# Frequency 0 as a bias in the last inverse transform's evictions: four products per row block instead of five

## The chip, the cores and the metric

The kernel runs on one core of a Trainium2 chip. The metric is the device time of one execution in microseconds; before the change the median of three runs is 128.48 us (128.36 to 128.61). In the profile PE is the matrix engine (TensorE), PEld its weight loads, DVE VectorE, ACT ScalarE, POOL GpSimd, and SP the engine that only issues transfers.

## The reference

The input x has 2048 rows (s) of 512 numbers (d). The output mixes two branches with one gate per row:

```python
    g = _sigmoid((x * gate_w).sum(-1, keepdims=True))
    a = _A_ref(x, A_w_r, A_w_i)
    b = _B_ref(x, B_w1, B_b1, B_w2, B_b2)
    return g * a + (1 - g) * b
```

Branch a is a spectral filter: a real 2-D Fourier transform over s and d, a product with a complex weight for each frequency pair (2048 x 257), and the inverse transform. Branch b is a token-mixing MLP: a layer norm over d, a product over s to 1792 hidden units, a gelu, a product back to 2048 rows with bias b2.

## The kernel before

All 2048 rows stay in SBUF as 16 blocks of 128 rows; block j = 4q + r holds the rows 512q + 4a + r. Fourier transforms are done as products with cosine and sine tables on TensorE, with radix-4 butterflies on VectorE around them, so that only short tables are needed. The MLP's products are m1 (line 727, x to hidden units, 14 tiles `ft`) and m2 (line 993, hidden units back to rows, 14 products of 128x512 per row block).

The stages in order: layer norm and the forward transform over s (i.e. fa, lines 584 to 587) between m1 products; the forward transform over d (fb, lines 692 to 695); the multiplication by the weights on VectorE; the inverse transform over s (i1, lines 893 to 900), between m2 products; a butterfly (fq, lines 928 and 929) that writes its result z in two halves h into the tile `xp` (`xph(0)` and `xph(1)`); and the last inverse transform, over d (i3, lines 975 to 979), for each row block j.

i3 uses the symmetry of cosines and sines: for a row block it makes four pieces in one PSUM bank: the even frequencies along d (h = 0) and the odd ones (h = 1) each give a cosine part and a sine part, for the first quarter of the columns d, from which the others follow by symmetry. The cosine part of h = 0 has 129 columns, the others 127, 128 and 128, 512 in all. The part v = 0 of z holds real parts, v = 1 imaginary parts. Frequencies 0 and 256 along d have no imaginary part, so frequency 256 is kept in the place of frequency 0's imaginary part. That is why the 129-column piece takes two products: one of the real parts with the cosine table, and a second, of the imaginary parts with a table in which only the row of frequency 256 is not zero (`g[:, 512:641]`).

The PSUM tiles of i3 alternate between the tags `fa` and `fb`, each with two buffers. ACT evicts each (i3ev, line 983), multiplying by the row's gate `g`, into a pair tile of `E` (`epair`, five pairs). Then VectorE adds and subtracts the pieces (`es`, `fold`, lines 998 to 1004) to get 512 outputs per row. For the first 14 row blocks ACT evicts m2's result with scale 1 − g and bias (1 − g) b2 (yev, line 1009; the four PSUM buffers of tag `acc`), and VectorE adds the two branches for a pair of blocks (`fin`, line 1023). For blocks 14 and 15 `es` adds the bias itself to the 129 columns of the cosine part (line 1028), and VectorE reads m2's result directly (`fin`, line 1035). A transfer on SP stores each group of rows.

The order of instructions isn't written by hand. Each step is a task with an engine, an estimated duration, what it reads and writes and a priority (`add`); `Plan.order` plays through the tasks with these estimates and emits them in the order in which they would start. So another estimate moves m2 products to other places between the transform's products. On each engine instructions run in that order. Transfers of SP and ACT use eight semaphore lanes; a ninth waits for the first on its lane.

Of the kernel before, what the change touches and what calls it, by code (L numbers as in the profile page):

```python
# [12 lines left out]
Alu = mybir.AluOpType  # L13
# [22 lines left out]
def make_tables():  # L36

    p = np.arange(P)
    r4 = np.arange(4)
    alt = np.where(p % 2 == 0, 1.0, -1.0)  # L40

    def ang(rows, k, n):
        return 2 * np.pi * ((rows[..., None] * k) % n) / n

    ta = np.zeros((P, 4, 640))
    ti = np.zeros((P, 2946))
    for r in range(4):
        s = 4 * p + r
        for n, k0 in enumerate((0, 2)):
            th = ang(s, k0 + 4 * np.arange(64), S)  # L50
            ta[:, r, n * 128:n * 128 + 64] = np.cos(th)
            ta[:, r, n * 128 + 64:n * 128 + 128] = -np.sin(th)
        ta[:, r, 64] = alt
        th = ang(s, 1 + 4 * p, S)
        ta[:, r, 256:384] = np.cos(th)
        ta[:, r, 384:512] = -np.sin(th)
        ta[:, r, 512:640] = -np.cos(th)

        k = 4 * (p % 64) + 2 * (p // 64)
        o, w = ti_at(r)  # L60
        v = ti[:, o:o + w]
        if r % 2:
            sg = np.where(p < 64, 1.0, -1.0)[:, None]
            th = ang(k, s, S)
            v = v.reshape(P, 7, P)
            v[:, 0] = np.cos(th)
            v[:, 1] = sg * np.cos(th)
            v[:, 2] = -np.sin(th)
            v[:, 3] = -sg * np.sin(th)
            v[0, 2:4] = alt * (0.5 ** 0.5 if r == 1 else -(0.5 ** 0.5))  # L70
            th = ang(1 + 4 * p, s, S)
            v[:, 4] = -np.sin(th)
            v[:, 5] = np.cos(th)
            v[:, 6] = np.sin(th)
            ti[:, o:o + w] = v.reshape(P, w)
        else:
            s5 = np.append(s, 512)
            for lt, kk in enumerate((k, 1 + 4 * p)):
                th = ang(kk, s5, S)
                c, n = np.cos(th), -np.sin(th)  # L80
                if lt == 0:
                    n[0, 0:P] = 0.0 if r == 0 else -alt
                u = v[:, 256 * lt:256 * lt + 256]
                u[:, 0:P], u[:, P:] = c[:, 0:P], n[:, 0:P]
                if r == 0:
                    u[:, P] = c[:, P] if lt == 0 else -n[:, P]
    ti[0, 2816:2945] = np.append(alt, 1.0)

    tb = np.zeros((P, 3, 4, 64))
    i = np.arange(64)  # L90
    for b in (0, 2):
        th = ang(p, b + 4 * i, D)
        tb[:, 0, b // 2] = np.cos(th)
        tb[:, 1, b // 2] = -np.sin(th)
    tb[:, 1, 0, 0] = alt
    tb[:, 2, 0:2] = tb[:, 0, 0:2]
    tc = np.zeros((P, 2, 3, 2, 64))
    for n, b in enumerate((1, 3)):
        th = ang(p, b + 4 * i, D)
        sg = 1.0 if b == 1 else -1.0  # L100
        tc[:, 0, 0, n] = np.cos(th)
        tc[:, 0, 1, n] = -np.sin(th)
        tc[:, 1, 0, n] = -sg * np.sin(th)
        tc[:, 1, 1, n] = -sg * np.cos(th)
    tc[:, :, 2] = tc[:, :, 0]
    cf = np.zeros((P, 4, 2))
    m = np.arange(8).reshape(4, 2)
    for r in range(4):
        cf[m[0, 0], r, 0] = 1.0
        cf[8, r, 0] = (1.0, -1.0)[r % 2]  # L110
        cf[m[1, r % 2], r, 0] = (1.0, -1.0, -1.0, 1.0)[r]
        if r != 2:
            cf[m[2, 0], r, 1], cf[m[3, 0], r, 1] = 1.0, (1.0, -1.0)[r % 2]
        if r != 0:
            cf[m[2, 1], r, 1], cf[m[3, 1], r, 1] = (0.0, -1.0, 1.0, 1.0)[r], (0.0, -1.0, -1.0, 1.0)[r]
    tb = np.concatenate([tb[:, :, 0:2].reshape(P, 384), tc.reshape(P, 768), cf.reshape(P, 8)], 1)

    tg = np.zeros((P, 642))
    sc = 2.0 / (D * S)
    d = np.arange(129)  # L120
    for h in range(2):
        th = ang(2 * p + h, d, D)
        c, n = sc * np.cos(th), -sc * np.sin(th)
        if h == 0:
            c[0], n[0] = sc / 2, 0.0
            tg[:, 0:129], tg[:, 129:256] = c, n[:, 1:128]
        else:
            tg[:, 256:384], tg[:, 384], tg[:, 385:512] = c[:, 0:128], -n[:, 128], n[:, 1:128]
    tg[0, 512:641] = np.where(d % 2 == 0, 1.0, -1.0) * sc / 2
    m, e = np.arange(P)[:, None], np.arange(3, -1, -1)  # L130
    ix = np.zeros((P, 2, 4))
    ix[:, 0] = 512 * e + 256 + np.where(m < 64, 4 * (64 - m), 4 * (127 - m) + 2)
    ix[0, 0] = (0, 1536, 1792, 1280)
    ix[:, 1] = 512 * e + 4 * (127 - m) + 3
    return {"ta": bf(ta), "ti": bf(ti), "tb": bf(tb), "tg": bf(tg), "tn": bf(np.eye(NFT)), "ix": ix.reshape(P, 8).astype(np.int32)}
# [142 lines left out]
def kernel(  # L278
# [39 lines left out]
    def dma(out_ap, in_ap, eng=None):  # L318
        (eng or nc.sync).dma_start(out=out_ap, in_=in_ap)
# [158 lines left out]
    def ld_ti():  # L478
        t["ti"] = sb([P, 2946], BF16, "rot")
        dma(t["ti"][:], tabs["ti"], nc.gpsimd)  # L480
    load("tg", [P, 642], BF16, tabs["tg"], (P, 1284), prio=120, eng="POOL", reads=[("hold", 3)])


    OWN = {0: (0, 8, 4, 12), 1: (1, 5), 2: (2,), 3: (3,)}
# [304 lines left out]
    for lt in range(2):  # L789
# [8 lines left out]
        if lt == 0:  # L798
            def nyq():
                pz = sb([1, 1280], F32, "X")  # L800
                na = pz[:, 0:1024].rearrange("p (i v l) -> p i v l", i=2, v=2)
                nn = t["nn"] = pz[:, 1024:1280].bitcast(BF16).rearrange("p (v l) -> p v l", v=2)
                wn, v = t["wn"], t["B"][0:1, 0, 0, 2:4, :]
                for i in range(2):
                    V.tensor_mul(na[:, i], v, wn[:, i, None, 0:L].to_broadcast([1, 2, L]))
                V.tensor_sub(nn[:, 0], na[:, 0, 1], na[:, 1, 0])
                V.tensor_add(nn[:, 1], na[:, 1, 1], na[:, 0, 0])
                V.tensor_mul(nn[:, :, 0], t["c0"][0:1, 0, 0, 1, :], wn[:, 0, 0:257:256])
            add("DVE", 3 * d1(512) + 0.1, nyq, reads=bk + [("W", 0), ("W", 1), ("c0", 0)] + pbk, writes=["nn"], prio=0.5)

        def c0b(lt=lt):
# [35 lines left out]
        add("DVE", tt(2048) + 2 * tt(1024), ob, reads=["xs"], writes=bk, prio=pr)  # L847

        def c0c(lt=lt):
            V.tensor_copy(t["B"][:, lt, :, :, 0], t["ce"][:, lt].rearrange("p e c k -> p e (c k)"))  # L850
        add("DVE", 0.15, c0c, reads=[("ce", lt)], writes=bk, prio=pr)

        if lt == 0:
# [76 lines left out]
        add("DVE", 2 * tt(2048), fq, reads=[("zz", h, r, lt) for r in range(4) for lt in range(2)] + [("T", 0, 0), ("T", 0, 1), ("T", 1, 0), ("T", 1, 1)], writes=["xs" if h == 0 else "pp", ("z", h)], prio=3.6)  # L930


    for i in range(NW):
        n = (0, 3, 5)
        if i in n:
            k = n.index(i)

            def w2alloc(k=k):
                t["w2", k] = sb([P, 6, S], BF16, "wa") if k == 0 else sb([P, 4, S], BF16, "wb", 2)
            add("SP", 0.01, w2alloc, writes=[("w2a", k)], prio=31 + i, alloc=["wa" if k == 0 else "wb"])  # L940

        def ldw2(i=i):
            w, o = w2at(2 * i)
            dma(w[:, o:o + 2, :], w2v[:, 2 * i:2 * i + 2, :])
        add("SP", 0.43, ldw2, reads=[("w2a", k)], writes=[("w2", i)], prio=31 + i, pk=(256, 5200))

    def w2at(ft):
        k = w1of(ft)
# [17 lines left out]
    for grp in groups:  # L966
        for j in grp:
# [3 lines left out]
            def i3(j=j, q=q, r=r, tag=tag):  # L971
                p3 = t["i3", j] = ps([P, 2, L], F32, tag, 2)
                g = t["tg"]
                zv = [xph(h).rearrange("p (q v r a) -> p q v r a", q=4, v=2, r=4)[:, q, :, r, :] for h in range(2)]
                T.matmul(p3[:, 0, 0:129], lhsT=zv[0][:, 0], rhs=g[:, 0:129], start=True, stop=False)
                T.matmul(p3[:, 0, 0:129], lhsT=zv[0][:, 1], rhs=g[:, 512:641], start=False, stop=True)
                T.matmul(p3[:, 0, 129:256], lhsT=zv[0][:, 1], rhs=g[:, 129:256], start=True, stop=True)
                T.matmul(p3[:, 1, 0:128], lhsT=zv[1][:, 0], rhs=g[:, 256:384], start=True, stop=True)
                T.matmul(p3[:, 1, 128:256], lhsT=zv[1][:, 1], rhs=g[:, 384:512], start=True, stop=True)
            add("PE", mm(*[129] * 5), i3, reads=[("z", 0), ("z", 1), "tg"], writes=[("i3", j)], prio=4, alloc=[tag])  # L980

            def i3ev(j=j):
                A.activation(epair(j // 2 % NEO)[:, j % 2], t["i3", j][:], ActF.Copy, scale=t["g"][:, j:j + 1])  # L983
            i3e = add("ACT", act(512, 1), i3ev, reads=[("i3", j), "g"], writes=[("eo", j)], prio=1.5, alloc=["eo"] if j % 2 == 0 else (), free=[tag],
                      after=[i3e] if j % 2 else ())
            parts = [slice(0, D)] if j < NJ - 1 else [slice(0, 384), slice(384, D)]
            for n, cs in enumerate(parts):
# [37 lines left out]
            else:  # L1025
                def es(j=j, fold=fold, quart=quart):
                    e, s = epair(j // 2 % NEO)[:, j % 2], espair()[:, :, 0:2]
                    V.tensor_scalar_add(e[:, 0, 0:129], e[:, 0, 0:129], t["ombb2"][:, j:j + 1])
                    fold(e, quart(tbuf(j)[:, None]), s)
                add("DVE", tiny(1) + 4 * tt(256) + 0.15, es, reads=[("eo", j), "omg"], writes=[("o", j)], prio=4, free=["eo"] if j % 2 else (), after=gates)  # L1030

                for n, cs in enumerate(parts):
                    def fin(j=j, n=n, cs=cs):
# [46 lines left out]
```

## Time and profile before

| | |
|---|---|
| median of 3 runs | 128.48 us (128.36 to 128.61) |
| the profiled execution | 128.45 us, its span 126.5 us |
| PE busy | 121.8 us, 746 products |
| DVE busy | 109.2 us |
| ACT busy | 81.4 us, 170 instructions |
| i3: L975 to L979 | 80 products, from 98.09 us on |
| i3ev: L983 | 16 of 128x512, about 0.71 us each |
| yev: L1009 | 14 of 128x512, 0.78 us each |
| the last four products of i1 (L893) | from 93.34 us on |
| the last eight products of PE (L993) | from 123.16 us on |

A span is the time from the first to the last recorded instruction; the execution's time holds 1.95 us more. Rows of the timeline give the start, the time from the first start to the last end, engine, line, operation, tiles and shapes, and the count of merged instructions. Matmuls follow each other before the one ahead has left the array, and ACT's instructions overlap too, so the step from one start to the next says what one costs its engine; the duration says when its result is there.

### The profile page before, as it was taken

The numbers are of one execution on the slowest core, as the hardware profiler recorded it, in microseconds if no ns is written. First come the engines' busy times: TensorE is split into PE (matmuls) and PEld (weight loads), VectorE is DVE, ScalarE is ACT, GpSimd is POOL, SyncE is SP. The second block draws the span as 40 slices with busy tenths as digits, with TensorE's granted clock in tenths as the row PEclk, the third lists the DMA queues.
The fourth block names the chain that finished last, engine by engine and source line by source line (L and its number), as shares of the span: only waits on it lengthen the run. The fifth ranks groups of instructions, "written<-read, shape, count | busy, mean of one in ns | idle before, by whom it ended". The sixth has DMA issues, their size and how long they took to land.

```text
span 126.5 us, 2104 instructions
## 1 busy us (share of the span) xinstructions
PE 121.8 (96%) x746; PEld 69.3 (55%) x759; DVE 109.2 (86%) x240; ACT 81.4 (64%) x170; POOL 28.0 (22%) x38
## 2 busy tenths in 40 slices
PE   6999999999999999999999999999999999999991
PEld 2455545565444476644455545557675776555570
DVE  1799999999999999999999999996597399999431
ACT  3799996999988889984220064228992999622200
POOL 6902638787778400000000000000000000000000
PEclk9999999999999999999999999999999999999999
DMA  4999999999999999991029600000000004213131
GB/s 99 323 349 369 364 369 364 335 337 341 296 211 207 341 392 416 408 387 56 0 21 372 274 0 0 0 3 8 0 0 0 5 0 166 95 71 139 47 110 41
DMA packets 15059, 23.14 MB, mean 183 GB/s; under 512 B 1496, under 2 KB 12138, under 8 KB 15050
## 3 DMA queue, kind: packets, MB, share of 16 engines
q1 hardware_dynamic: 13338, 19.70, 47.4%
q0 software_dynamic: 1232, 2.91, 7.1%
q10 hardware_dynamic: 480, 0.40, 0.9%
q8 instruction: 6, 0.10, 0.4%
q14 instruction: 3, 0.02, 0.1%
HBM read 20.90 MB, written 2.10 MB: 182 GB/s over the span
## 4 chain that ended last, share of the span: by engine, by line
PE 92%; DMA 3%; ACT 1%; issue 1%; SPq 0%; DVE 0%
PE acc L993 37%; PE acc L727 32%; PE fb L727 5%; DMA wa<-in_B_w_dram 3%; PE fb L695 1%; PE fa L587 1%; PE fa L893 1%; PE fa L586 1%; PE fb L893 1%; PE fa L695 1%; PE fa L584 1%; PE fa L585 1%; PE fa L993 1%; ACT X L983 1%; PE fa L692 0%
## 5 line engine op out<-in xcount | busy, mean ns | idle before, releaser
L993 PE MATMUL acc<-gl,wb 128*128 128x512 bf16 (+1 forms) x124 | 31.1, 376 | 0.1
L727 PE MATMUL acc<-h,wb 128*128 128x512 bf16 x124 | 28.6, 379 | 0.2
L993 PE MATMUL acc<-gl,wa 128*128 128x512 bf16 (+1 forms) x94 | 24.0, 376 | 0.2
L993 PEld LDWEIGHTS <-wb 128*128 128x128 bf16 x136 | 14.7, 114 | 10.6 <-issue 0.2
L727 PEld LDWEIGHTS <-wb 128*128 128x128 bf16 x128 | 12.5, 98 | 13.9
L1009 ACT ACTIVATE x<-acc,ombb,omg 128x512 bf16<-128x512 f32 x14 | 10.7, 776 | 14.7 <-PE acc L993 14.7
L727 PE MATMUL acc<-h,wa 128*128 128x512 bf16 (+1 forms) x66 | 16.7, 366 | 0.2 <-DMA wa<-in_B_w_dram 0.2
L993 PEld LDWEIGHTS <-wa 128*128 128x128 bf16 x102 | 11.1, 113 | 8.4
L727 PEld LDWEIGHTS <-wa 128*128 128x128 bf16 x102 | 9.8, 98 | 9.0 <-DMA wa<-in_B_w_dram 1.0
L747 ACT ACTIVATE gl<-acc,b1f 128x512 bf16<-128x512 f32 x12 | 8.0, 690 | 7.6 <-PE acc L727 7.6
L494 DVE BATCH_NORM_STATS2 stats<-x 128x6 f32<-128x512 bf16 x12 | 8.2, 682 | 2.2 <-DMA x<-in_A_x_dram 2.2
L467 POOL DMA_INDIRECT W<-in_A_w_r_dram,ix x8 | 9.4, 1171 | 2.4 <-issue 2.4
L763 ACT ACTIVATE x<-x 128x512 bf16<-128x512 bf16 x16 | 9.9, 621 | 0.0
L727 PE MATMUL fb<-h,wa 128*128 128x512 bf16 (+1 forms) x33 | 9.6, 366 | 0.1
L590 ACT CAST X<-fa 128x512 bf16<-128x512 f32 x16 | 9.0, 575 | 1.1 <-PE fa L587 0.9
L467 POOL DMA_INDIRECT W<-in_A_w_i_dram,ix x8 | 8.8, 1101 | 2.4 <-issue 2.4
L555 ACT ACTIVATE h<-x,nmr,rstd 128x512 bf16<-128x512 bf16 x8 | 6.4, 806 | 0.0
L864 ACT CAST s<-fa 8x512 bf16<-8x512 f32 x1 | 0.6, 574 | 8.3 <-PE fa L862 8.3
L983 ACT ACTIVATE X<-fb,g 128x512 bf16<-128x512 f32 x8 | 5.7, 708 | 0.0
L983 ACT ACTIVATE X<-fa,g 128x512 bf16<-128x512 f32 x8 | 5.6, 706 | 0.0
L699 ACT CAST B<-fa 128x512 bf16<-128x512 f32 x8 | 5.0, 624 | 0.6 <-PE fa L695 0.6
L1023 DVE TENSOR_TENSOR x<-x,X 128x1024 bf16<-128x1024 bf16 x7 | 4.6, 685 | 0.8 <-ACT x L1009 0.8
(177 smaller groups left out, 245.7 us busy)
## 6 DMA issues: line engine op xcount, KB each, us to landing
wb<-in_B_w_dram SPq DMA_DIRECT2D x8, 512.0 KB, 12.7
wb<-in_B_w_dram SPq DMA_DIRECT2D x4, 1024.0 KB, 8.7
wa<-in_B_w_dram SPq DMA_DIRECT2D x3, 1024.0 KB, 10.7
wa<-in_B_w_dram SPq DMA_DIRECT2D x2, 768.0 KB, 8.6
out_dram<-x SPq DMA_DIRECT2D x3, 512.0 KB, 3.7
x<-in_A_x_dram SPq DMA_DIRECT2D x2, 512.0 KB, 9.3
wa<-in_B_w_dram SPq DMA_DIRECT2D x4, 192.0 KB, 4.2
wa<-in_B_w_dram SPq DMA_DIRECT2D x2, 384.0 KB, 5.0
```

What stands on the lines that cost most here:

```text
L467: add("POOL", 1.0, lambda lt=lt, e=e: nc.gpsimd.indirect_dma_start(out=W()[:, lt, e, 1, 0:257], out_offset=None, in_=w, in_offset=bass.Ind ...
L494: V.bn_stats(out=t["stats"][:, j, :], in_=t["x"][:, j // 4, j % 4, :])
L555: add("ACT", act(512, 2), lambda j=j: A.activation(t["h"][:, j // 4, j % 4, :], t["x"][:, j // 4, j % 4, :], ActF.Identity, bias=t["nmr"][ ...
L590: add("ACT", act(512), lambda r=r, dq=dq: A.copy(t["X"][:, :, r, :, dq, :], t["pa", r, dq][:]), reads=[("pa", r, dq)], writes=[("X", r, dq ...
L699: A.copy(t["B"][:, lt, e, 2 * c:2 * c + 2, :].rearrange("p s (i b) -> p s i b", b=4), t["pb", lt, e, c][:].rearrange("p s b i -> p s i b"))
L727: T.matmul(t["u", ft][:, cs], lhsT=w[:, j // 4, j % 4, c * P:(c + 1) * P], rhs=t["h"][:, j // 4, j % 4, cs], start=(j == jorder[0] and not ...
L747: gelus.append(add("ACT", act(512, 1), lambda ft=ft: A.activation(t["gl"][:, ft, :], t["u", ft][:], ActF.Gelu_apprx_tanh, bias=t["b1f"][:, ...
L763: A.activation(t["x"][:, q, r, :], t["x"][:, q, r, :], ActF.Copy, accum_out=t["glog"][:, 4 * q + r:4 * q + r + 1])
L983: A.activation(epair(j // 2 % NEO)[:, j % 2], t["i3", j][:], ActF.Copy, scale=t["g"][:, j:j + 1])
L993: T.matmul(t["y", j, n][:, cs], lhsT=w[:, o, 512 * q + r:512 * q + 512:4], rhs=t["gl"][:, ft, cs], start=(ft == 0), stop=(ft == NFT - 1))
L1009: A.activation(tbuf(j).rearrange("p h d -> p (h d)"), t["y", j, 0][:], ActF.Identity, bias=t["ombb2"][:, j:j + 1], scale=t["omg"][:, j:j + 1])
L1023: V.tensor_add(o, o, epair(NEO + 1 + j // 2 % NOB))
```

## The change

Frequency 256 takes the place of frequency 0 in the first row of the cosine table, so that the 129-column piece needs one product. For that the two change places in z: the copies of the lines' end values (`c0c`) and the row of frequency 1024 along s (`nyq`) are written in reversed order. What frequency 0 along d adds is the same number in all 129 columns of a row's cosine part. It is brought into one number per row: a transfer (`dcl`, 4 x 512 from one partition of `xph(0)` to the tile `dc`), four small products with a unit matrix that turn it into columns (`dct`), and two VectorE operations (`dcs`) that multiply by the gate and, for blocks 14 and 15, add the bias of b2. ACT's eviction becomes two: 383 columns with scale g as before, and the 129 columns of the cosine part with scale g and bias `dcb`. Line 1028 goes. The w2 tiles 1 and 2 come in one transfer instead of two.

In the new order TensorE's instructions are the same up to the last L893; after it come 11 products of line 993, `dct`, 8 more, four i3 blocks in a row, and then the other twelve blocks after 5, 3, 3, 3, 3, 7, 3, 3, 7, 3, 3 and 7 products of line 993. Before, it was 20 products, four blocks, and then one or two products between blocks for most of them. On VectorE, each pair's `es` is followed by its `fin`; before, two of the one came ahead of two of the other.

```diff
-    tg = np.zeros((P, 642))
+    tg = np.zeros((P, 512))
...
-            c[0], n[0] = sc / 2, 0.0
+            c[0], n[0] = np.where(d % 2 == 0, 1.0, -1.0) * sc / 2, 0.0
...
-    tg[0, 512:641] = np.where(d % 2 == 0, 1.0, -1.0) * sc / 2
...
-                V.tensor_mul(nn[:, :, 0], t["c0"][0:1, 0, 0, 1, :], wn[:, 0, 0:257:256])
+                V.tensor_mul(nn[:, ::-1, 0], t["c0"][0:1, 0, 0, 1, :], wn[:, 0, 0:257:256])
...
-            V.tensor_copy(t["B"][:, lt, :, :, 0], t["ce"][:, lt].rearrange("p e c k -> p e (c k)"))
+            V.tensor_copy(t["B"][:, lt, :, :, 0].rearrange("p e (c v) -> p e c v", c=2)[:, :, :, ::-1], t["ce"][:, lt])
...
+    def dcl():
+        t["dc"] = sb([4, D], BF16, "dc")
+        dma(t["dc"][:], xph(0)[0:1].rearrange("p (q v n) -> p q v n", q=4, v=2)[:, :, 1], DCE)
+    DCE = None
+    add("SP", 0.5, dcl, reads=[("z", 0)], writes=["dc"], prio=0, pk=(4, 1024, 4))
+
+    def dct():
+        pd = t["pdc"] = ps([P, 4, 4], F32, "fb", 2)
+        for r in range(4):
+            T.matmul(pd[:, r], lhsT=t["dc"][:, r * P:(r + 1) * P], rhs=t["tn"][0:4, 0:4], start=True, stop=True)
+    add("PE", 0.2, dct, reads=["dc", "tn"], writes=["pdc"], prio=2.9, alloc=["fb"])
+
+    def dcs():
+        v = lambda name: t[name][:].rearrange("p (q r) -> p r q", r=4)
+        t["dcb"] = sb([P, NJ], F32, "dcb")
+        V.scalar_tensor_tensor(v("dcb"), t["pdc"][:], 1.0 / (D * S), v("g"), op0=Alu.mult, op1=Alu.mult)
+        V.tensor_add(t["dcb"][:, 14:16], t["dcb"][:, 14:16], t["ombb2"][:, 14:16])
+    add("DVE", 0.25, dcs, reads=["pdc", "g", "omg"], writes=["dcb"], prio=1, free=["fb"], after=gates)
+
-    for i in range(NW):
+    for i, e in ((0, 1), (1, 3), (3, 4), (4, 5), (5, 6), (6, NW)):
...
-                T.matmul(p3[:, 0, 0:129], lhsT=zv[0][:, 0], rhs=g[:, 0:129], start=True, stop=False)
-                T.matmul(p3[:, 0, 0:129], lhsT=zv[0][:, 1], rhs=g[:, 512:641], start=False, stop=True)
+                T.matmul(p3[:, 0, 0:129], lhsT=zv[0][:, 0], rhs=g[:, 0:129], start=True, stop=True)
...
-            add("PE", mm(*[129] * 5), i3, reads=[("z", 0), ("z", 1), "tg"], writes=[("i3", j)], prio=4, alloc=[tag])
+            add("PE", mm(*[129] * 4), i3, reads=[("z", 0), ("z", 1), "tg"], writes=[("i3", j)], prio=4, alloc=[tag])
...
-                A.activation(epair(j // 2 % NEO)[:, j % 2], t["i3", j][:], ActF.Copy, scale=t["g"][:, j:j + 1])
-            i3e = add("ACT", act(512, 1), i3ev, reads=[("i3", j), "g"], writes=[("eo", j)], prio=1.5, alloc=["eo"] if j % 2 == 0 else (), free=[tag],
+                e = epair(j // 2 % NEO)[:, j % 2].rearrange("p h d -> p (h d)")
+                v = t["i3", j][:].rearrange("p h d -> p (h d)")
+                A.activation(e[:, 129:], v[:, 129:], ActF.Copy, scale=t["g"][:, j:j + 1])
+                A.activation(e[:, 0:129], v[:, 0:129], ActF.Identity, bias=t["dcb"][:, j:j + 1], scale=t["g"][:, j:j + 1])
+            i3e = add("ACT", act(383, 1) + act(129, 2), i3ev, reads=[("i3", j), "g", "dcb"], writes=[("eo", j)], prio=1.5, alloc=["eo"] if j % 2 == 0 else (), free=[tag],
...
-                    V.tensor_scalar_add(e[:, 0, 0:129], e[:, 0, 0:129], t["ombb2"][:, j:j + 1])
```

More of the change, by code (lines that the diff above doesn't have):

```diff
@@ L480, in ld_ti @@
         dma(t["ti"][:], tabs["ti"], nc.gpsimd)
-    load("tg", [P, 642], BF16, tabs["tg"], (P, 1284), prio=120, eng="POOL", reads=[("hold", 3)])
+    load("tg", [P, 512], BF16, tabs["tg"], (P, 1024), prio=120, eng="POOL", reads=[("hold", 3)])
     OWN = {0: (0, 8, 4, 12), 1: (1, 5), 2: (2,), 3: (3,)}
@@ L940, with ldw2 @@
             add("SP", 0.01, w2alloc, writes=[("w2a", k)], prio=31 + i, alloc=["wa" if k == 0 else "wb"])
-        def ldw2(i=i):
+        def ldw2(i=i, n=2 * (e - i)):
             w, o = w2at(2 * i)
-            dma(w[:, o:o + 2, :], w2v[:, 2 * i:2 * i + 2, :])
-        add("SP", 0.43, ldw2, reads=[("w2a", k)], writes=[("w2", i)], prio=31 + i, pk=(256, 5200))
+            dma(w[:, o:o + n, :], w2v[:, 2 * i:2 * i + n, :])
+        add("SP", 0.43, ldw2, reads=[("w2a", k)], writes=[("w2", m) for m in range(i, e)], prio=31 + i, pk=(256 * (e - i), 5200))
     def w2at(ft):
@@ L1027, in es @@
                     e, s = epair(j // 2 % NEO)[:, j % 2], espair()[:, :, 0:2]
-                    V.tensor_scalar_add(e[:, 0, 0:129], e[:, 0, 0:129], t["ombb2"][:, j:j + 1])
                     fold(e, quart(tbuf(j)[:, None]), s)
-                add("DVE", tiny(1) + 4 * tt(256) + 0.15, es, reads=[("eo", j), "omg"], writes=[("o", j)], prio=4, free=["eo"] if j % 2 else (), after=gates)
+                add("DVE", tiny(1) + 4 * tt(256), es, reads=[("eo", j)], writes=[("o", j)], prio=4, free=["eo"] if j % 2 else (), after=gates)
                 for n, cs in enumerate(parts):
```

## The prediction

> **What bounds the kernel now.** I read the page first, then the chain of waits, then the timeline of the stretch that the diff touches, and last the rows that price its new instructions.
>
> ```profile
> span 126.5 us, 2104 instructions
> PE 121.8 (96%) x746; PEld 69.3 (55%) x759; DVE 109.2 (86%) x240; ACT 81.4 (64%) x170; POOL 28.0 (22%) x38
> ...
> PE 92%; DMA 3%; ACT 1%; issue 1%; SPq 0%; DVE 0%
> ```
>
> TensorE ends the chain nearly everywhere. A 96% average can hide a stage with another limit, so the table by stretches for the last third:
>
> ```profile
> 98.10:107.50 9.40, 9.24 (x102) 6.90 (x103) 7.11 (x22) 9.40 (x17) 0.00 (x0) 1.00 0.14 58
> 107.50:123.80 16.30, 16.22 (x89) 9.20 (x88) 11.95 (x36) 4.38 (x7) 0.00 (x0) 1.00 0.23 89
> ```
>
> After the length come PE, PEld, DVE, ACT, POOL with counts, then the granted clock. In the first stretch, where the last transform runs, two engines are full: PE with 9.24 of 9.40 us and ACT with 9.40. So a gain on PE is real only if the change doesn't push ACT past it. The order of work shows the rhythm:
>
> ```profile
> 103.33 0.22 PE L975 MATMUL fa<-tg,xp 128*128 128x129 bf16 x1
> 103.38 0.22 PE L976 MATMUL fa<-tg,xp 128*128 128x129 bf16 x1
> ...
> 103.61 0.38 PE L993 MATMUL acc<-gl,wb 128*128 128x512 bf16 x1
> ...
> 103.82 0.22 PE L975 MATMUL fb<-tg,xp 128*128 128x129 bf16 x1
> ```
>
> Starts count, since matmuls overlap: five products take 103.61 − 103.33 = 0.28 us, 0.056 each; one L993 takes 0.216 (1.46 us for six from 108.47 to 109.76 gives 0.215).
>
> **What goes.** One of five products (L976) in 16 row blocks: 16 × 0.056 = 0.90 us of PE. Two L1028 additions on DVE (0.25 each) go too. DVE isn't on the path there: in the end it waits 1.52 us for L993 before L1035, so I count nothing. The one PE gap in the stretch (the fifth block starts at 99.49, 0.06 after the L993 from 99.22 could end) waits for the first eviction. In the new order five L993 stand ahead of that block, not one, so it goes: 0.06.
>
> **What comes on PE.** Four tiny products (dct, 4x128 weights, 4 columns). The trace has their twins, L708, behind L706:
>
> ```profile
> 19.15 0.38 PE L727 MATMUL acc<-h,wa 128*128 128x512 bf16 x1
> 19.47 0.18 PE L706 MATMUL fa<-tn,b1b 14*128 14x14 bf16 x1
> 19.50 0.26 PE L708 MATMUL fa<-tn,b2b 4*128 4x4 bf16 x4
> 19.70 0.39 PE L727 MATMUL acc<-h,wa 128*128 128x512 bf16 x1
> ```
>
> The L727 from 19.15 frees PE at 19.37 and the next starts at 19.70: 0.33 for five, of which 0.20 from 19.50 are the four. Bounds 0.20 and 0.33; four added products gain nothing. I take 0.30, as the 0.10 gap ahead comes with such a group.
>
> **The wait for dc.** dct needs a transfer that starts when the first half of z is done:
>
> ```profile
> 92.10 1.22 DVE L929 TENSOR_TENSOR xp<-X 128x2048 bf16<-128x2048 bf16 x1
> ```
>
> That is 93.32, so issue at 93.4. PE's order up to the last L893 is unchanged; those are through at 93.78, then come eleven L993 (11 × 0.2157 = 2.37) to 96.15, and there dct stands, with all later products queued behind it. So the transfer has 2.75 us. The nearest row is B<-s, 8 KB between SBUF tiles on SP (dc is 4 KB): issued at 82.31, read by the weight load of L897 at 84.92, which had not waited for it, so at most 2.61. The small stores land 1.5 and 1.6 us after issue. The far row is s<-X with 4.8, issued at 67.2 while the w2 loads moved 372 GB/s; around 93 nothing moves. I take 2 us: hidden, cost nothing. On SP's queue only the output stores stand behind it, the first at 104.7.
>
> Then dcs: two small DVE operations (0.17 each, as L713 and L771) behind the last L929, which ends at 97.26. dcb is there at 97.7, and the first ACT instruction that reads it comes after 99. Hidden by over 1 us.
>
> **The split eviction, the step that decides.** 16 × L983 (512 columns, one pointer) become 383 columns with one pointer plus 129 with two. Again I read starts:
>
> ```profile
> 103.31 0.74 ACT L983 ACTIVATE X<-fa,g 128x512 bf16<-128x512 f32 x1
> 103.88 0.75 ACT L983 ACTIVATE X<-fb,g 128x512 bf16<-128x512 f32 x1
> 104.52 0.78 ACT L1009 ACTIVATE x<-acc,ombb,omg 128x512 bf16<-128x512 f32 x1
> 105.20 0.68 ACT L983 ACTIVATE X<-fa,g 128x512 bf16<-128x512 f32 x1
> ```
>
> So 0.57 for L983 and 0.68 for L1009, which has the second half's form. Neither width is in the trace. The slope per column comes from one operand form at two widths: L498, one column with a bias pointer, 0.19 from start to start (two take 0.48, one 0.29), and L747, 512 columns with a bias pointer, 0.58 (three take 1.85, one 0.69): 0.39 / 511 = 0.76 ns. Then 383 columns: 0.57 − 129 × 0.00076 = 0.47; 129 columns: 0.68 − 383 × 0.00076 = 0.39; pair 0.86. Bounds: 1.25 if narrower saves nothing; 0.77 if the 0.475 from start to start of the L908 casts were columns alone (0.93 ns).
>
> What PE allows: in the new order the blocks stand mostly three L993 apart, 4 × 0.056 + 3 × 0.2157 = 0.87 us, and three times seven apart, 1.73, where ACT also does one L1009 (0.86 + 0.68 = 1.54). Two PSUM tiles per tag let PE be four blocks ahead. So 0.86 fits in 0.87, by a hair. The start: dct to 96.45, eight L993 to 98.18, four blocks to 99.07, five L993 to 100.15; ACT begins row 8's L1009 at 98.38, the first pair at 99.06, and has it written at 100.0, in time. ACT therefore costs 0, though it stays full to about 116 us instead of 110.
>
> The Trainium skill, "ScalarE: Activation LUTs", section "What ACT_TABLE_LOAD costs", speaks against the split: a fixed 186 ns per instruction, 0.833 ns a column, 93 ns a pointer, 93 ns overlap. By it the pair is estimated at 0.51 + 0.39 = 0.89, 0.02 over the 0.87; the stretches of seven give most of it back, and the sum would be about 0.05 worse.
>
> **DVE.** es and its addition now alternate, from about 100.9: seven pairs of 1.73 (100.05 to 101.78 now) and 0.65 for L1023 (two take 1.29), two single rows of 1.01 (1.30 less the L1028): 18.7 us, to 119.6. Row 14's L1035 could begin at 120.1 and delays the end only if it begins after 121.6 (row 15's, at 123.03 now, less 0.66 and its own 0.75). Cost 0, with 2 us in hand.
>
> **The rest.** One w2 load of 2 MB for two of 1 MB: these are issued at 37.3 to 40.9 and first read at 64.8, so nothing. tg is 32 KB shorter, nothing. The reversed copies in c0c and nyq (0.21 and 0.16) might gain or lose 0.1 each; PE has L993 products to do and reaches the first transform product that reads them with 0.9 us in hand.
>
> **Sum.** −0.90 − 0.06 + 0.30 = −0.66. The profiled execution took 128.45 (span 126.5 and 1.95 around it), close to the median 128.48. Forecast 127.8.
>
> **Rivals.**
> 1. *ACT becomes the bound: slower.* If the two halves don't overlap as neighbours do now (0.74 us each, 0.57 apart), the pair costs its durations: 0.706 − 0.10 + 0.776 − 0.29 = 1.09. Then each of eight blocks three apart waits 0.22, the fifth 0.15: 1.9 us, and 127.8 + 1.9 = 129.7. It decides from a pair of about 0.97. Against it: every pair of neighbours in the timeline overlaps by 0.1 or more, whatever the form. 9%.
> 2. *ACT is a little too slow: no change.* With a pair of 0.93 to 0.97, waits of 0.3 to 0.65 eat the gain: 128.1 to 128.45. For it: the fit is a hair wide. 10%.
> 3. *dc comes late.* With s<-X's 4.8 us it lands at 98.2, PE stands 2.05 us: 129.9. It costs from 2.75 us of latency on. Against it: DMA is idle there. 5%.
> 4. *The products were hidden anyway*, so that the change doesn't do what it says: no change, 128.5. Against it: of 25.70 us in the two stretches PE is idle 0.24. 2%.
>
> **The numbers.** The forecast's case has 74%, by itself 127.5 (dct 0.20, less the 0.13 by which the runs of before lie off their median, rounded down) to 128.1 (dct 0.33, a pair of 0.91, and the same 0.13). Faster means over 0.2%, below 128.22, about what a measurement here can tell: 74% and a third of rival 2, 77%. Same: the rest of 2 and rival 4, 9%. Slower: rivals 1 and 3, 14%. The range reaches from there to rival 2's end, 127.5 to 128.5, and leaves out rivals 1 and 3 with 14%.
>
> **What would show it.** Right: no idle of PE at the new blocks in the waits; pair to pair on ACT at most 0.87; PE's last L993 ending about 0.65 us sooner; 0.3 us between the L993 on either side of dct; dc landed before 96.1. Wrong: PE waiting for ACT's 129-column half (rivals 1 and 2), PE or PEld waiting for dc (rival 3), or L1035 starting late behind DVE's chain.

## The result and the profile after

The changed kernel takes 128.06 us in the median of 10 runs (127.58 to 128.80), the kernel before 128.56 in the runs beside it: a ratio of 0.9952, 95% interval 0.9933 to 0.9971. A second set of runs gave 0.9927 (0.9908 to 0.9946). The forecast was 127.8 in a range of 127.5 to 128.5, faster. The profiled execution took 127.62 us against 128.45. The page of the changed kernel, where lines past the new functions have moved (L993 is now L1013, L983 is L1002 and L1003):

```profile
span 125.8 us, 2092 instructions
PE 121.4 (96%) x734; PEld 68.4 (54%) x747; DVE 109.4 (87%) x240; ACT 85.3 (68%) x186; POOL 27.6 (22%) x38
...
PE 96%; issue 1%; DVE 0%
```

PE still ends the chain. The ACT share that the chain had, the first evictions ahead of the fifth block, is gone. The rest of the rise from 92% to 96% isn't the change: before, 3% were a transfer of `wa` in the first 5 us, ahead of everything that the change touches. The two stretches of the last third, in the same columns as before:

```profile
98.10:107.50 9.40, 9.29 (x78) 6.11 (x79) 6.53 (x18) 8.68 (x19) 0.00 (x0) 1.00 0.13 54
107.50:123.80 16.30, 15.52 (x97) 9.22 (x96) 12.78 (x38) 9.03 (x20) 0.00 (x0) 1.00 0.24 92
```

In the first, PE is busy for 9.29 of 9.40 us and ACT now has room (8.68). ACT's work has moved into the second stretch, 9.03 us where there were 4.38. The lower PE share in the second stretch isn't idle time between products: PE is done there before 123.8.

A span also holds the first half of the kernel, which differs by some tenths between executions of code that is the same. So I measure the change inside the trace, from the start of the first forty m2 products (a row of the chain) to the start of VectorE's last operation. Before:

```profile
64.79 8.63 PE acc L993 x40
...
123.81 0.35 DVE x L1035
```

and after:

```profile
64.71 8.63 PE acc L1013 x40
...
123.11 0.35 DVE x L1054
```

That is 123.81 − 64.79 = 59.02 us before and 58.40 after: 0.62 us less, against 0.66 in the forecast's sum. Two more executions of the changed kernel gave 58.40 and 58.41. All experiments are read by this stretch, with "behind it" the time from its end to the end of the span:

| kernel | stretch, us | against the changed kernel | behind it, us |
|---|---|---|---|
| before | 59.02 | +0.62 | 2.7 |
| changed | 58.40 | | 2.7 |
| products_alone | 58.16 | −0.24 | 2.7 |
| no_dc | 58.10 | −0.30 | 2.8 |
| fifth_back | 59.28 | +0.88 | 2.7 |
| old_estimate | 60.73 | +2.33 | 2.7 |
| four_pieces | 60.76 | +2.36 | 2.7 |
| dct_early | 59.05 | +0.65 | 2.7 |
| one_product | 58.33 | −0.07 | 3.0 |
| one_transfer | 58.34 | −0.06 | 2.7 |
| full_rows | 58.14 | −0.26 | 2.7 |

The runs one_transfer, the first full_rows and after_third come from a chip on which the kernel before, too, took a median of 141.91 us; what was lost lies ahead of the stretch, in which the granted clock is 1.00, and only the stretch and what follows it is read from them.

### The profile page after: what moved, and what is told of

It is laid out like the page before. It is cut to its first block, busy times and chain, and to the rows that moved or that the text cites. A ratio compares the mean times of both kernels' runs of the same rounds, so it can differ in the third digit from the quotient of the medians.

```text
span 125.8 us, 2092 instructions
## 1 busy us (share of the span) xinstructions
PE 121.4 (96%) x734; PEld 68.4 (54%) x747; DVE 109.4 (87%) x240; ACT 85.3 (68%) x186; POOL 27.6 (22%) x38
## 4 chain that ended last, share of the span: by engine, by line
PE 96%; issue 1%; DVE 0%
PE acc L1013 38%; PE acc L726 33%; PE fb L726 5%; PE fa L368 3%; PE fa L585 1%; PE fb L694 1%; PE fb L892 1%; PE fa L694 1%; PE fa L892 1%; PE fa L586 1%; PE fa L583 1%; PE fa L584 1%; PE fa L1013 1%; PE fa L993 0%; PE fa L691 0%
## 5 line engine op out<-in xcount | busy, mean ns | idle before, releaser
L1013 PE MATMUL acc<-gl,wb 128*128 128x512 bf16 (+1 forms) x123 | 31.2, 376 | 0.2
L1013 PE MATMUL acc<-gl,wa 128*128 128x512 bf16 (+1 forms) x95 | 23.9, 376 | 0.1
L1013 PEld LDWEIGHTS <-wb 128*128 128x128 bf16 x136 | 14.4, 114 | 10.2 <-DMA wb<-in_B_w_dram 0.2
L1013 PEld LDWEIGHTS <-wa 128*128 128x128 bf16 x102 | 11.0, 113 | 8.2
L698 ACT CAST B<-fb 128x512 bf16<-128x512 f32 x8 | 5.1, 634 | 0.0
L1043 DVE TENSOR_TENSOR x<-x,X 128x1024 bf16<-128x1024 bf16 x7 | 4.8, 690 | 0.2
L368 PE MATMUL fa<-xp 128*128 128x512 bf16 x9 | 4.0, 631 | 1.0 <-DVE eps L330 1.0
```

What stands on the lines that cost most here:

```text
L368: T.matmul(pw[:].rearrange("p (a n) -> p a n", a=4), lhsT=t["warm"], rhs=t["warm"][:, None, :].to_broadcast([P, 4, P]), start=True, stop=True)
L698: A.copy(t["B"][:, lt, e, 2 * c:2 * c + 2, :].rearrange("p s (i b) -> p s i b", b=4), t["pb", lt, e, c][:].rearrange("p s b i -> p s i b"))
L1013: T.matmul(t["y", j, n][:, cs], lhsT=w[:, o, 512 * q + r:512 * q + 512:4], rhs=t["gl"][:, ft, cs], start=(ft == 0), stop=(ft == NFT - 1))
L1043: V.tensor_add(o, o, epair(NEO + 1 + j // 2 % NOB))
```

## The experiments

The theory: the fifth product was on the path and pays 0.056 us sixteen times; dct costs 0.3 us there; ACT's second instruction costs nothing, because the new order leaves it 0.87 us per block. Rivals: the gain comes from the new order or the shorter DVE work; or the split costs something that the gain covers up.

### The products without the rest

```diff
-                T.matmul(p3[:, 0, 0:129], lhsT=zv[0][:, 0], rhs=g[:, 0:129], start=True, stop=False)
-                T.matmul(p3[:, 0, 0:129], lhsT=zv[0][:, 1], rhs=g[:, 512:641], start=False, stop=True)
+                T.matmul(p3[:, 0, 0:129], lhsT=zv[0][:, 0], rhs=g[:, 0:129], start=True, stop=True)
```

made in the kernel before, with the planner's estimate for four products.

> The kernel before with nothing changed but the fifth product of each row block left out (so what frequency 256 adds is missing from the output); evictions, DVE and transfers as before. Theory (PE is the bound, one product costs it 0.056 us): 16 x 0.056 = 0.90 us and the 0.06 us gap go, nothing comes in their place: a profiled span of 125.5 to 125.7 against 126.5, a ratio of about 0.9925. Rival (the gain of the change comes from the new spacing of the blocks and not from the products): 126.2 to 126.5, ratio 0.998 to 1.0.

The median was 127.55 us, a ratio of 0.9927 (0.9902 to 0.9952), as expected; the span, 126.2, missed the expected 125.6, because this execution started m2 late, at 65.31 us:

```profile
65.31 8.63 PE acc L992 x40
...
123.47 0.35 DVE x L1034
```

By the stretch it is 58.16, 0.86 less than before (0.96 were expected). About half of what is missing is the gap at the fifth block, which did not go: with two m2 products ahead of it, PE is free at 99.97 and the block starts at 100.02. So the products were on the path, with the old evictions and with most blocks two m2 products apart.

### The changed kernel without frequency 0's way

```diff
-    def dcl(): ...
-    def dct(): ...
-    def dcs(): ...
...
-                A.activation(e[:, 0:129], v[:, 0:129], ActF.Identity, bias=t["dcb"][:, j:j + 1], scale=t["g"][:, j:j + 1])
+                A.activation(e[:, 0:129], v[:, 0:129], ActF.Identity, bias=t["ombb2"][:, j:j + 1], scale=t["g"][:, j:j + 1])
```

> The changed kernel without the transfer dc, the four products dct and the two DVE operations dcs; the 129-column half takes its bias from another tile of the same shape that is there anyway (so what frequency 0 adds is missing from the output). Theory: it gives back the 0.28 us that dct takes on PE and nothing else, a span of about 125.5 against 125.8 of the changed kernel; the split evictions cost nothing, so it ends with products_alone within 0.1. Rival (the split also costs time somewhere): it stays 0.2 us or more above products_alone.

```profile
64.99 8.63 PE acc L994 x40
...
123.09 0.35 DVE x L1035
```

58.10 us: 0.30 less than the changed kernel, which is dct's whole price, and no more than products_alone (58.16), which has one eviction instruction per block. So the split costs nothing that the stretch shows. (The 0.06 by which it is shorter is about the gap that products_alone keeps.) The ratio to the kernel before was 0.9937 (0.9916 to 0.9959).

### The fifth product back

```diff
-                T.matmul(p3[:, 0, 0:129], lhsT=zv[0][:, 0], rhs=g[:, 0:129], start=True, stop=True)
+                T.matmul(p3[:, 0, 0:129], lhsT=zv[0][:, 0], rhs=g[:, 0:129], start=True, stop=False)
+                T.matmul(p3[:, 0, 0:129], lhsT=zv[0][:, 1], rhs=g[:, 512:641], start=False, stop=True)
```

> The changed kernel with a fifth product in each row block again, against a table of zeros, in the same order of instructions: split, dc, dct and dcs stay. Theory: 16 x 0.056 = 0.90 us more than the changed kernel: a span of 126.7 against 125.8, no faster than the kernel before (126.5), the 0.2 to 0.3 above it being dct. Rival (the new order or the shorter DVE work brought the gain): within 0.3 us of the changed kernel.

```profile
64.94 8.63 PE acc L1014 x40
...
124.22 0.35 DVE L1055 SCALAR_TENSOR_TENSOR x<-fa,omg,x 128x128 bf16<-128x128 f32 x1 [0.16 <-PE fa L1014]
```

The stretch grows by 0.88 us, 0.055 for each product, to 0.26 more than before. The ratio to the kernel before is 1.0018 (0.9990 to 1.0046). With the new order, the split and the shorter DVE work in place and only the product count restored, the whole gain is gone: the rival that credits the order or DVE falls.

### The order of before, by the old estimate

```diff
-            i3e = add("ACT", act(383, 1) + act(129, 2), i3ev, ...
+            i3e = add("ACT", act(512, 1), i3ev, ...
```

> The changed kernel, but the planner is told the old duration for the eviction (one instruction of 512 columns), so it places the row blocks mostly two products of line m2 apart and not three; the instructions are the same, only their order differs. Theory (the reordering is what hides ScalarE's two instructions): pairs take 0.81 us on ScalarE, a block with two m2 products 0.66 on PE, so from the fifth block on PE waits for PSUM buffers: the 16th block can start at 98.99 + 12 x 0.81 + 0.68 + 0.16 = 109.5 us, PE's own work would bring it there at 107.3, so about 2.1 us are lost: a span of 127.8 to 128.0. Rival (four PSUM buffers give enough room, the order does not matter): 125.8.

The median is 130.02 us, a ratio of 1.0120 (1.0090 to 1.0150): the same instructions, 1.2% slower than the kernel before. Its timeline on PE (start, length, engine, line, operation; the rest of each block's products left out):

```profile
99.20 0.59 PE L1013 MATMUL acc<-gl,wa 128*128 128x512 bf16 x2
99.93 0.22 PE L993 MATMUL fa<-tg,xp 128*128 128x129 bf16 x1
...
100.16 0.59 PE L1013 MATMUL acc<-gl,wa 128*128 128x512 bf16 x2
100.75 0.22 PE L993 MATMUL fb<-tg,xp 128*128 128x129 bf16 x1
...
104.85 0.22 PE L993 MATMUL fa<-tg,xp 128*128 128x129 bf16 x1 [0.22 <-ACT X L1003]
```

Two m2 products from 100.16 on take 0.43, so PE could go on at 100.59 and goes on at 100.75. The blocks come 0.82 us apart, the pace of ACT's pairs, where PE would need 0.66. The last line names what it waits for: the 129-column half. The 16th block starts at 109.62 (109.5 were expected) and 2.33 us are lost (2.1 expected; the span of 128.1 is 0.1 above the expected top). So ACT's extra instruction is hidden by the spacing that the planner made from the new estimate, and by that alone; four PSUM buffers don't do it.

### ScalarE past its room

```diff
-                A.activation(e[:, 129:], v[:, 129:], ActF.Copy, scale=t["g"][:, j:j + 1])
+                for lo, hi in ((129, 257), (257, 385), (385, 512)):
+                    A.activation(e[:, lo:hi], v[:, lo:hi], ActF.Copy, scale=t["g"][:, j:j + 1])
```

> The changed kernel with the 383-column eviction cut into three (128, 128 and 127 columns), in the same order on PE: ScalarE's four pieces of a block should take 3 x 0.25 + 0.345 = 1.09 us against the 0.87 that PE leaves. Theory: ScalarE becomes the bound of the stretch: PE waits about 0.22 us at each of eight blocks and a little at four more, 2.1 us in all: a span of 127.7 to 128.0. Rival (ScalarE's share is still hidden, the buffers take it up): below 126.2.

```profile
99.05 0.87 ACT L1003 ACTIVATE X<-fa,g 128x128 bf16<-128x128 f32 x3
99.80 0.48 ACT L1004 ACTIVATE X<-fa,dcb,g 128x129 bf16<-128x129 f32 x1
100.14 0.90 ACT L1003 ACTIVATE X<-fb,g 128x128 bf16<-128x128 f32 x3
```

From block to block ACT takes 100.14 − 99.05 = 1.09 us, as expected, and the stretch is 2.36 us longer (2.1 expected; the span of 128.3 is 0.3 above the expected top). The ratio is 1.0118 (1.0092 to 1.0143). This is rival 1 of the prediction made real: a block time of 1.09 on ACT turns the change into a loss of 1.2%. The rival's price, 1.9 us, was 0.46 too low.

### When dc lands

```diff
-    add("PE", 0.2, dct, reads=["dc", "tn"], writes=["pdc"], prio=2.9, alloc=["fb"])
+    add("NOP", 0.1, lambda: None, reads=[("z", 0)], writes=["dcgo"])
+    add("PE", 0.2, dct, reads=["dcgo", "tn"], writes=["pdc"], prio=-1, alloc=["fb"])
```

> The changed kernel with dct placed after three m2 products behind the last L892 and not after eleven, at about 94.4 us, so that PE has to wait for the transfer dc and shows when it lands (issued at 93.3). Theory: it lands 1.5 to 2.6 us after issue, at 94.8 to 95.9: PE waits 0.4 to 1.5 us, a span of 126.2 to 127.3, and at its place in the changed kernel (96.1) it has 0.2 us or more in hand. Rival (the transfer takes 4.8 us as s<-X did): PE waits 3.7 us, a span of 129.5, and the changed kernel would have to show a wait of 2 us, which would have to be hidden by a missing record.

The chain now runs through the transfer:

```profile
93.71 1.78 DMA dc<-xp
95.49 0.05 issue
95.54 0.25 PE fb L941 x4
```

1.78 us from issue to landing. In the changed kernel dc is issued at 93.27 and so there at about 95.05 (an estimate with the same 1.78), while dct stands at 96.17: 1.1 us in hand. Here PE stood idle for 0.58 us and the stretch grew by 0.65. Rival 3 (4.8 us) falls. The Trainium skill, "DMA: Bandwidth & Descriptors", section "Anatomy of one DMA — SWDGE (gpsimd) path", gives about 2.0 us of fixed cost for a transfer that GpSimd issues; this one, issued on SP, took 0.2 less.

### One product instead of four

The changed kernel's dct, on PE's timeline:

```profile
94.78 1.46 PE L1013 MATMUL acc<-gl,wa 128*128 128x512 bf16 x6
96.17 0.25 PE L941 MATMUL fb<-tn,dc 4*128 4x4 bf16 x4
96.35 1.92 PE L1013 MATMUL acc<-gl,wb 128*128 128x512 bf16 x8
```

Six m2 products from 94.78 free PE at 96.07. dct starts at 96.17, the next m2 product at 96.35: 0.28 us, of which 0.10 is a gap ahead. The row of eight behind it lasts 1.92 where the same row takes 1.89 elsewhere, which makes up the 0.30 of no_dc. Four products are needed only because dc lies as 4 x 512. The first attempt lays it out as 16 x 128 by four transfers:

```diff
-        for r in range(4):
-            T.matmul(pd[:, r], lhsT=t["dc"][:, r * P:(r + 1) * P], rhs=t["tn"][0:4, 0:4], start=True, stop=True)
+        T.matmul(pd[:], lhsT=t["dc"][:], rhs=t["tn"][:], start=True, stop=True)
```

> A version that should beat both: dc is laid out as 16 x 128 by four small transfers, so that one product against a 16 x 16 unit matrix gives all 16 columns, and one product instead of four stands on PE (it is placed four m2 products later, since the four transfers take longer to issue). Theory: dct's 0.28 us on PE becomes 0.06 for the product and the 0.10 gap ahead of it, 0.16 in all: 0.1 us less than the changed kernel, a span of 125.7, if the last of the four transfers lands before 96.9 us; if each takes 0.7 us to issue it lands at about 97.7 and PE waits 0.8: 126.5.

```profile
97.14 0.18 PE L941 MATMUL fb<-tn,dc 16*128 16x16 bf16 x1
97.24 0.58 PEld L1012 LDWEIGHTS <-wb 128*128 128x128 bf16 x4
97.25 1.05 PE L1012 MATMUL acc<-gl,wb 128*128 128x512 bf16 x4
```

PE is free at 97.04 here, dct starts at 97.14 and the next m2 product at 97.25: 0.21 us for one product, not the 0.16 expected, since there is a gap behind it as well. The m2 product's own weight load isn't done ahead either: it starts at 97.24. So PE gained only 0.07 in the stretch, and the profiled span was 126.2; the median of 128.13 (0.9946, 0.9925 to 0.9967) isn't below the changed kernel's 127.80 beside it. 0.3 us were lost behind the stretch (3.0 against 2.7). The waits on SP show where: the longest wait for an output store at the end is 0.6 us, in the kernel before 0.3. The next version changes the layout of z instead, so that one transfer does it:

```diff
-            z = xph(h).rearrange("p (q v n) -> p q v n", q=4, v=2)
+            z = xph(h).rearrange("p (v q n) -> p q v n", q=4, v=2)
...
+        dma(t["dc"][0:NJ], xph(0)[0:1, 2048:4096].rearrange("p (k a) -> p k a", a=P), DCE)
```

> As one_product, but z is laid out so that frequency 0's 2048 numbers lie in one row, and one transfer brings them into 16 x 128: one transfer, one product, and the last store on the same semaphore lane as in the kernel before. Measured inside the trace, from the start of the first forty m2 products to the start of the last VectorE instruction (59.02 us before, 58.40 after the change, 58.33 in one_product): 58.33. If the 0.35 us that one_product's execution lost behind its last store came from its four transfers and shifted lanes, it is gone here: a span 0.1 below the changed kernel's, 125.7. If it came with the one product, it stays: 126.1.

The stretch is 58.34 us, with 2.7 behind it, and the longest wait for a store is 0.3 again. So the loss at the end came with the four transfers, not with the one product; whether by their number or by the shifted semaphore lanes isn't told apart.

### The gaps around dct

```diff
+        t["dc"] = sb([P, P], BF16, "dc")
+        V.memset(t["dc"][:], 0.0)
...
-"tn": bf(np.eye(NFT))
+"tn": bf(np.eye(P, NJ))
```

on top of one_transfer: the transfer still fills 16 rows, the other 112 are zeros.

> As one_transfer, with dc and the unit matrix filled up to 128 rows by zeros, so that the product has the 128 x 128 weights that all its neighbours have. Theory (the gaps of 0.1 us before and behind dct come from the weights with few rows, which aren't loaded ahead): the weight load runs ahead of time, the gaps go, dct costs 0.06 in all, and the stretch takes 58.40 - 0.28 + 0.06 = 58.18 us, next to products_alone (58.16) and no_dc (58.10). Rival (the gaps come from the wait for the transfer or from the change of tile): 58.33 as in one_transfer.

> full_rows once more, since in its first runs the kernel before too took over 130 us on that chip: the stretch from the first forty m2 products to the last VectorE instruction again 58.14 us, 0.26 below the changed kernel; a median 0.2 to 0.3 below the changed kernel's, a ratio to the kernel before of 0.991 to 0.993.

The stretch was 58.14 us in both. PE in the second of them, then its weight loads:

```profile
95.07 1.24 PE L1012 MATMUL acc<-gl,wa 128*128 128x512 bf16 x5
96.15 0.17 PE L941 MATMUL fb<-tn,dc 128*128 128x16 bf16 x1
96.18 0.39 PE L1012 MATMUL acc<-gl,wa 128*128 128x512 bf16 x1
```

```profile
95.94 0.10 PEld L941 LDWEIGHTS <-dc 128*128 128x128 bf16 x1
```

Five m2 products from 95.07 end at 96.15, and there dct starts, without a gap; 0.03 us later PE goes on. The weight load ran at 95.94, while the last m2 product was still at work. In the changed kernel the 4-row loads start at 96.17 together with their products, after an idle time of 0.41. So the gap is the weight load that isn't done ahead, and it belongs to weights with few rows: the transfer was there in both. one_transfer has dct at the same place in the order, with 16 rows: PE is free at 112.82, its weight load starts at 112.91 and the product at 112.92, and the next m2 product only at 113.03. Between the two kernels only dc and the unit matrix, filled up with zeros, differ. This version is the fastest of the study that leaves nothing out of the output: a median of 127.61 us (127.36 to 127.88), 0.9914 of the kernel before (0.9887 to 0.9940). Against the changed kernel the stretch shows 0.26 us, about what the totals can tell apart. A third set of runs of the changed kernel stood beside the first full_rows:

> The changed kernel beside the two others: 58.40 us in that stretch, ratio to the kernel before 0.993 to 0.995.

Its stretch was 58.41; the expected ratio isn't read from that set. The other repeated set:

> The changed kernel once more, on the chip and beside the runs of the next one: ratio to the kernel before 0.995, span 125.8 to 126.3.

It gave 127.80 us, the 0.9927 named above, and a span of 125.8.

## Why the prediction was right

**The bound.** PE was the bound, with ACT beside it: products_alone gained 0.86 us by itself, fifth_back took the whole gain away.

**The products.** Forecast 0.90 and 0.06 for the gap; measured 0.88 (fifth_back against the changed kernel) and 0.92 in all (no_dc against before). The gap went, as forecast: the fifth block starts at 100.09, where the five m2 products ahead of it end. Starts as the price, not the 0.22 us that each row shows, were the right reading: 16 × 0.22 would have been 3.5.

**dct.** Forecast 0.30 from the five products of L706 and L708, bounds 0.20 and 0.33; measured 0.30 by no_dc, 0.28 on the timeline. The gap ahead came along, as in the twin, whose weights have few rows too. The forecast took it over without a cause, so that it hit exactly is partly luck.

**dc.** Forecast hidden, 2 us of latency with 2.75 to spend; measured 1.78.

**The split.** Forecast a pair of 0.86 against 0.87, with bounds of 0.77 and 1.25. The changed kernel's ACT:

```profile
98.99 0.57 ACT L1002 ACTIVATE X<-fa,g 128x383 bf16<-128x383 f32 x1
99.45 0.46 ACT L1003 ACTIVATE X<-fa,dcb,g 128x129 bf16<-128x129 f32 x1
99.79 0.59 ACT L1002 ACTIVATE X<-fb,g 128x383 bf16<-128x383 f32 x1
100.26 0.48 ACT L1003 ACTIVATE X<-fb,dcb,g 128x129 bf16<-128x129 f32 x1
100.60 0.60 ACT L1002 ACTIVATE X<-fa,g 128x383 bf16<-128x383 f32 x1
```

0.46 and 0.34, a pair of 0.81 (100.60 − 99.79). So the step had more room than forecast: 0.06 for each block, not 0.01. What was off was the slope per column: 0.76 ns from L498 and L747, whereas L983 to L1002 shows (0.57 − 0.46) / 129 = 0.85 and L1009 to L1003 (0.68 − 0.34) / 383 = 0.89. The one-column row reads SBUF and the other PSUM, so their fixed parts may differ; no run here tests that. The Trainium skill, "ScalarE: Activation LUTs", section "What ACT_TABLE_LOAD costs", has 0.833 ns a column, which the slopes agree with within 0.06. Estimated with that page's fixed parts the two would take 0.51 and 0.39, 0.05 more each than these evictions from PSUM took.

**DVE.** Forecast from 100.9 to 119.6, with 2 us in hand; measured from 100.77 to 119.07 (the last L1043 starts at 118.39 and takes 0.68), where L1054 then waits 0.98 us for PE.

**The chances and the range.** Rivals 1 and 2 did not come about, as the pair was 0.81; four_pieces and old_estimate show that the mechanism is real. Its price at 1.09 was forecast as 1.9 us and came out as 2.36. A pair of 0.93 to 0.97, rival 2's, was not tried. Rival 3 needed 2.75 us of latency and met 1.78. Rival 4 falls with fifth_back. Too small was the spread of runs that I took over from the three of before (0.13 to either side): the ten runs of the changed kernel reach from 127.58 to 128.80, beyond the top of the range, and their median lies 0.26 above the forecast, though the profiled execution lies 0.18 below it. The ratio, 0.48% below 1, is the forecast's 0.66 us (0.51%) within its interval.

## What to carry to other kernels

Where two engines are full in the same stretch, price what is taken from the one and what is put on the other by start-to-start times, and compare the sums per repeating unit: 0.81 us of ACT against 0.87 of PE decided here, and the same instructions in a tighter order lost 2.33 us. Where a planner sets the order, a new duration in its table is as much part of the change as the instruction. In these runs a small product in a full PE stream cost least when its weights had the same full shape as its neighbours': 0.03 us with 128 rows, mostly zeros, against 0.21 for one with 16 rows and 0.28 to 0.30 for four with 4 rows.

## What the runs showed of the hardware

The load of weights with 4 rows (or 16, in one_product and one_transfer) was not done ahead of time, that of 128 rows was; it cost 0.10 us ahead of the product. The full load that follows such a one wasn't done ahead either, which left the next product 0.11 us behind the 16-row one, where it follows the filled one by 0.03. I had taken the 0.10 us over from the L706 row without knowing its cause. And a product of 128x16 against 128x128 weights took 0.03 us from start to start, less than the 0.056 of the 128-column ones. Four small transfers on SP in place of one came with 0.3 us more behind the start of the last VectorE operation, in the wait for the last output stores; of this the cause is open.
